# A fused attention and token-MLP kernel on one core: GpSimd library switches moved, head outputs of later query blocks in freed weight space, task order by deadlines

## The chip, the core and the metric

The kernel runs on one core of a Trainium2 chip. The metric is the device time of one execution in microseconds (us). Most executions of one kernel agree within 0.3%; a difference under 2% is called "same".

Engines: TensorE (PE; its weight loads are PEld), VectorE (DVE), ScalarE (ACT), GpSimd (POOL), SyncE (SP, which issues nearly all DMAs). The granted clock is the share of full speed at which TensorE was allowed to run; "half clock" means 0.5.

## The reference

```python
x = A_x                                   # 1 x 2048 x 512, bf16
xn = layernorm(x)                         # over the last axis, no scale
A: qkv = xn @ wqkv; 32 heads of 16; softmax(q k^T / 4) v; then @ wo
B: h = layernorm(xn); u = gelu(h^T @ w1 + b1)   # mixes tokens: 2048 -> 1376
   y = u @ w2 + b2                              # 1376 -> 2048
return x + A + B^T
```

## The kernel before

The kernel is written as a small scheduler. It holds a modelled time for each engine, and picks the next score, exponential, value product or MLP piece by estimate; what it emits is a fixed order of instructions on each engine. So one changed cost or due date moves work everywhere.

The attention has 1024 exponentials of 128x1024. ScalarE does some directly (720 before). VectorE does the others as an integer trick: one pass from PSUM, then three shifted copies, made by VectorE or by GpSimd (`int64_add`). Such an exponential needs four value products on TensorE in place of one.

`affine_select` at the start and `int64_add` in the main loop live in different GpSimd libraries; a switch is put ahead of an instruction whose library may not be resident.

```python
# head: GpSimd
ident.memset(0); affine_select(ident, ...)      # standard library
mhalf.memset(-0.5) ...                          # needed by every rstd (pow)

def late_consts():                              # ahead of the main loop
    pool: memset(wo_t)
    # ... 12 DMAs of wo; those of wo_t wait for the memset
    pool: b1col <- b1c_bf

oT = sb("oT", [128, 2, 4, 512], BF16)           # head outputs, query block % 2

def task_epilogue(b):                           # after the value products of a block
    # ... copy out of PSUM, denominators through DRAM and back to denb
    yield "gate", lambda: qb < 2 or all(("f", 4 * (qb - 2) + i) in have for i in range(4))
    # oT[:, qb % 2, T] = oC32 * denb            # VectorE

# tasks that fill TensorE between scores: Q, K, V projections, MLP in (ut), MLP out (fin)
KV_DUE = {1: BN + 8, 2: 170, 3: 236}            # due = number of the score
for T in range(1, 4):
    for c in range(4):
        ext_tasks.append((KV_DUE[T] - 8, KV_DUE[T] + KV_STEP * c, "kt", ...))
        # ... vt
for i in range(NFT):                            # UT_DUE, UT_STEP = 100, 38
    ext_tasks.append((due - UT_LEAD, due, "ut", ...))
for st in range(NT):                            # FIN_DUE = (500, 650, 800, 920)
    ext_tasks.append((due - 16, due, "fin", ...))
# cuts marked by "..."
```

A Q task ends with eight small DMAs that copy rows of `Qall` into `QT`, and the scores of the next blocks wait for these rows. All these tasks share one PSUM bank.

The softmax here doesn't subtract the row's maximum and nothing guards it: scores larger than these inputs give would overflow.

## Time and profile before

716.44 us (median of 3; 715.01 to 716.99). The profiled execution spans 715.6 us; its device time was 717.96 us, above these three.

| stretch (trace) | us |
|---|---|
| start to the first exponential on ScalarE | 19.86 |
| first to last exponential's start (the loop) | 684.29 |
| last exponential's start to the end (tail) | 11.49 |

Two engines are nearly always busy. These are the first lines of the profile's page (busy us and share of the span, number of instructions), and the chain of waits that ended last, by engine.

```profile
span 715.6 us, 29348 instructions
PE 688.3 (96%) x12863; PEld 315.3 (44%) x12867; DVE 622.7 (87%) x916; ACT 677.8 (95%) x739; POOL 382.6 (53%) x649
PE 67%; ACT 19%; DVE 7%; issue 2%; SPq 2%; POOL 1%; DMA 1%; DVEq 0%; POOLq 0%
```

Busy shares do not say what can be won, so I count starts: back to back, ScalarE starts an exponential every 0.904 us. 719 intervals of that length are 650.0 us, the gelu in the middle of the loop adds 8.1, and 26.2 of the 684.3 us are left. By this count that is what a better order could win at most without moving exponentials.

The head: GpSimd's timeline (start, duration, engine, line, operation, and in brackets the idle time before it with what ended it), then the records of line 396.

```profile
0.72 0.21 POOL L395 MEMSET ident<- 128x128 bf16 x1 [0.30 <-POOLq L1474]
8.72 0.28 POOL L396 TENSOR_SCALAR_AFFINE_SELECT ident<-ident 128x128 bf16<-128x128 bf16 x1 [7.79 <-issue]
8.97 0.09 POOL L399 MEMSET mhalf<- 128x1 f32 x1
```

```profile
L396 POOLq MODIFY_POOL_CONFIG  x2: 11/11/11, 1.1 to 1.2; - x2
```

The library switch itself takes 11 ns at 1.2 us, and then nothing runs on GpSimd for 7.5 us. "Issue" means that the profile shows nothing that was waited for. `mhalf` and all normalization stand behind it.

In the loop, the longest wait of ScalarE for a score (its timeline), and a second place where VectorE's queue stood still for the denominators of an earlier block (VectorE's timeline):

```profile
239.87 2.96 ACT L718 ACTIVATE pT<-ps 128x1024 bf16<-128x1024 f32 x3
247.42 2.13 ACT L718 ACTIVATE pT<-ps 128x1024 bf16<-128x1024 f32 x2 [4.58 <-PE ps L694]
```

```profile
316.15 0.89 DVE L988 TENSOR_TENSOR oT<-oC,denb 128x256 bf16<-128x256 f32 x2 [1.83 <-DMA denb<-rden_scratch]
```

Busy time by stretch around the second (stretch, length, busy us and count of PE, PEld, DVE, ACT, POOL, then granted TensorE clock, DMA share, GB/s):

```profile
315.00:320.00 5.00, 3.37 (x48) 0.88 (x40) 3.78 (x6) 3.19 (x4) 2.47 (x5) 0.90 0.08 20
320.00:325.00 5.00, 5.00 (x88) 2.35 (x88) 3.35 (x6) 3.39 (x4) 1.84 (x3) 0.76 0.05 8
```

TensorE ran dry behind VectorE, its granted clock then fell to half for 3.4 us, and ScalarE lost over 3 us in ten.

### The profile page before, as it was taken

The page shows a single profiled execution, that of the slowest core. Times are in us where ns is not written, and L with a number is a line of the kernel's source. Part 1 is how long each engine was busy: PE and PEld are TensorE (multiplying, and loading weights), DVE is VectorE, ACT ScalarE, POOL GpSimd, SP SyncE. Part 2 cuts the span into 40 slices and gives each one's busy share as a digit, 9 for nine tenths or more (in the row PEclk, how much of TensorE's full clock was granted, in tenths as well). Part 3 has the DMA queues.
Part 4 walks back from the last instruction along what each step waited for, and adds up shares of the span by engine and source line. Part 5 has one row for each costly group of instructions (what it writes and reads, how often), then busy time and mean ns, then how long its engine had stood idle before and what let it go on. Part 6 is the DMA issues. An engine that isn't in the chain of part 4 may idle for free.

```text
span 715.6 us, 29348 instructions
## 1 busy us (share of the span) xinstructions
PE 688.3 (96%) x12863; PEld 315.3 (44%) x12867; DVE 622.7 (87%) x916; ACT 677.8 (95%) x739; POOL 382.6 (53%) x649
## 2 busy tenths in 40 slices
PE   4999999999999999999999999999999999999998
PEld 2544444445444534434444444444444444444444
DVE  3889988998888789888989999997899889898897
ACT  2899999999999799989999999999999999999994
POOL 4454545554544255555656566664656556565662
PEclk7999999999999999999999999999999999999999
DMA  7103020220022121122103211212221222212111
GB/s 208 29 19 66 21 47 19 52 47 17 21 45 43 26 47 39 24 50 40 38 20 74 52 43 40 53 46 51 45 56 35 49 60 51 47 23 56 36 27 44
DMA packets 85728, 32.32 MB, mean 45 GB/s; under 512 B 67424, under 2 KB 85600, under 8 KB 85600
## 3 DMA queue, kind: packets, MB, share of 16 engines
q1 hardware_dynamic: 85168, 30.05, 18.4%
q8 instruction: 101, 1.65, 1.1%
q10 hardware_dynamic: 432, 0.39, 0.2%
q14 instruction: 27, 0.22, 0.1%
HBM read 21.76 MB, written 2.35 MB: 34 GB/s over the span
## 4 chain that ended last, share of the span: by engine, by line
PE 67%; ACT 19%; DVE 7%; issue 2%; SPq 2%; POOL 1%; DMA 1%; DVEq 0%; POOLq 0%
PE ps L761 26%; PE ps L694 24%; PE ps L791 14%; ACT pT L718 13%; ACT x_sb L718 5%; SPq L391 2%; DVE pT L729 2%; PE ps L840 1%; DMA denb<-rden_scratch 1%; DVE x_sb L729 1%; DVE hx L519 1%; ACT gT_sb L895 1%; DVE OT L951 1%; DVE pT L738 0%; DVE oT L988 0%
## 5 line engine op out<-in xcount | busy, mean ns | idle before, releaser
L718 ACT ACTIVATE pT<-ps 128x1024 bf16<-128x1024 f32 x522 | 509.2, 1118 | 9.6 <-PE ps L694 8.5
L694 PE MATMUL ps<-QT,KT 32*128 32x512 bf16 x2048 | 287.5, 385 | 6.5 <-ACT pT L718 2.8
L729 DVE TENSOR_SCALAR pT<-ps 128x1024 int16<-128x1024 f32 x216 | 263.8, 1222 | 28.1 <-PE ps L694 20.6
L735 POOL INT64_ADD pT<-pT x311 | 188.7, 615 | 158.6 <-DVE pT L738 90.8
L761 PE MATMUL ps<-pT,V 128*32 128x256 bf16 x4696 | 251.3, 275 | 2.5 <-DVE OT L951 1.2
L718 ACT ACTIVATE x_sb<-ps 128x1024 bf16<-128x1024 f32 x198 | 210.8, 1122 | 4.2 <-PE ps L694 3.7
L694 PEld LDWEIGHTS ps<-QT,KT 32*128 32x128 bf16 x2048 | 80.8, 91 | 182.5 <-ACT pT L718 69.8
L761 PEld LDWEIGHTS ps<-pT,V 128*32 128x32 bf16 x4696 | 114.5, 96 | 72.4 <-issue 50.9
L761 PE MATMUL ps<-x_sb,V 128*32 128x256 bf16 x1832 | 120.1, 276 | 1.8 <-DVE OT L951 0.8
L729 DVE TENSOR_SCALAR x_sb<-ps 128x1024 int16<-128x1024 f32 x88 | 107.5, 1222 | 9.8 <-PE ps L694 6.7
L735 POOL INT64_ADD pT<-x_sb x117 | 71.3, 617 | 55.4 <-DVE pT L738 40.0
L735 POOL INT64_ADD x_sb<-pT x113 | 69.2, 615 | 57.5 <-DVE pT L738 34.2
L738 DVE TENSOR_SCALAR pT<-pT 128x1024 int16<-128x1024 int16 x154 | 65.6, 428 | 4.6
L761 PEld LDWEIGHTS ps<-x_sb,V 128*32 128x32 bf16 x1832 | 47.4, 96 | 34.0 <-issue 22.9
L761 PE MATMUL ps<-pT,VM 128*32 128x256 bf16 x864 | 61.6, 275 | 0.6 <-DVE pT L738 0.6
L791 PE MATMUL ps<-gT_sb,wblk 128*32 128x512 bf16 (+1 forms) x704 | 60.0, 384 | 0.8 <-DMA wblk<-in_B_w_dram 0.7
L791 PE MATMUL ps<-hx,wblk 128*32 128x512 bf16 x688 | 59.8, 389 | 0.0
L735 POOL INT64_ADD x_sb<-x_sb x49 | 30.1, 618 | 26.8 <-DVE pT L738 15.2
L738 DVE TENSOR_SCALAR x_sb<-pT 128x1024 int16<-128x1024 int16 x70 | 29.7, 427 | 1.9
L738 DVE TENSOR_SCALAR pT<-x_sb 128x1024 int16<-128x1024 int16 x70 | 29.5, 425 | 1.8 <-PE ps L761 0.2
L761 PEld LDWEIGHTS ps<-pT,VM 128*32 128x32 bf16 x864 | 23.3, 96 | 12.4 <-issue 9.5
L761 PE MATMUL ps<-x_sb,VM 128*32 128x256 bf16 x352 | 25.3, 276 | 0.0
(103 smaller groups left out, 385.1 us busy)
## 6 DMA issues: line engine op xcount, KB each, us to landing
wblk<-in_B_w_dram SPq DMA_DIRECT2D x10, 512.0 KB, 4.5
wblk<-in_B_w_dram SPq DMA_DIRECT2D x16, 320.0 KB, 3.7
oC<-OT SPq DMA_DIRECT2D x248, 16.0 KB, 1.8
denb<-rden_scratch SPq DMA_DIRECT2D x124, 32.0 KB, 2.1
xr<-in_A_x_dram SPq DMA_DIRECT2D x16, 128.0 KB, 2.5
dcomp<-OT SPq DMA_DIRECT2D x124, 2.0 KB, 1.8
QT<-Qall SPq DMA_DIRECT2D x120, 16.0 KB, 1.9
out_dram<-osb SPq DMA_DIRECT2D x14, 128.0 KB, 1.8
```

Of the source, the lines that this page charges most:

```text
L391: return eng.dma_start(dst, src)
L519: return [dict(eng="dve", fn=lambda e: e.tensor_scalar(xn_sb[:, t, :], xn_sb[:, t, :], mv[:, t, 3:4], None, ALU.mult), reads=[("xn", t), ( ...
L694: specs.append(dict(eng="pe", fn=lambda e, r=r, bk=bk: e.matmul(bank(bk), lhsT=KT[32 * r:32 * r + 32, T, 128 * kt:128 * (kt + 1)], rhs=QT[ ...
L718: return [dict(eng="act", fn=lambda e: e.activation(buf(pbuf[n]), ps[:, s_ * 1024:(s_ + 1) * 1024], ACTF.Exp, scale=LN2_128), reads=[("ban ...
L729: return dict(eng="dve", fn=lambda e: e.tensor_scalar(buf_i(w), ps[:, s_ * 1024:(s_ + 1) * 1024], IBIAS, 0.0, ALU.add, ALU.max), reads=[(" ...
L735: return dict(eng=eng, fn=lambda e: e.int64_add(buf_i(o).bitcast(I64), buf_i(w).bitcast(I64), SHIFTS[k] * 0x0001000100010001), reads=[("pT ...
L738: return dict(eng=eng, fn=lambda e: e.tensor_scalar(buf_i(o), buf_i(w), float(SHIFTS[k]), 1.0, ALU.add, ALU.mult), reads=[("pT", w)], writ ...
L761: specs.append(dict(eng="pe", fn=lambda e, c=c, h=h, i=i, off=off: e.matmul(bank(PV_BANK)[32 * c:32 * c + 32, 256 * par:256 * par + 256], ...
L791: specs.append(dict(eng="pe", fn=lambda e, c=c, w=w: e.matmul(bank(EX_BANK)[32 * c:32 * c + w, :], lhsT=lhs_of(32 * c, 32 * c + w), rhs=rh ...
L840: specs.append(dict(eng="pe", fn=lambda e, ct=ct, c=c, i=i, t=t: e.matmul(bank(EX_BANK)[32 * c:32 * c + 32, 128 * i:128 * (i + 1)], lhsT=x ...
L895: yield "act", [dict(eng="act", fn=lambda e, ap=ap: e.activation(ap, ap, ACTF.Gelu_apprx_tanh), reads=[("gT", f) for f in fts], writes=[(" ...
L951: yield "pvev", [dict(eng="dve", fn=lambda e: e.tensor_copy(OT32[:, eb, :], bank(PV_BANK)), reads=[("bank", PV_BANK)], writes=[("OT32", eb)])]
```

## The change

The intent: leave the GpSimd with the library that the next execution needs first; do the other switch early; give head outputs of query blocks 2 and 3 their own place (the K and V weights, dead by then), so that they need not wait for the MLP output tasks; and choose the order of tasks from deadlines instead of fixed dates.

```diff
+    def load_lib(lib):
+        sc.add("pool", lambda e: e.load_library(lib), cost=(LIB_I, LIB_I), name="lib", port=False)   # LIB_I = 7.2
     def late_consts():
+        load_lib(INT64_LIB)
         sc.add("pool", lambda e: e.memset(wo_t[:], 0.0), ...)
 ...
-    oT = sb("oT", [128, 2, 4, 512], BF16)
+    oT_a = sb("oT", [128, 2, 4, 512], BF16)
+    oT_b = wkv_raw[:, :].rearrange("p (q t x) -> p q t x", q=2, t=4)
+    def oT(qb): return oT_a[:, qb] if qb < 2 else oT_b[:, qb - 2]
 ...
-    yield "gate", lambda: qb < 2 or all(("f", 4 * (qb - 2) + i) in have for i in range(4))
 ...
+    hard.append((2 * BN * p - Q_LEAD, 0.86, "qt", ...))            # and kt, vt: due = first use - lead
+    soft = [(3.42, "ut", ...)]; fins = [(3.2, "fin", ...)]         # put where the hard ones leave slack
 ...
-D_STEAL = 0.8
-D_LATE = 0.6
+D_STEAL = 0.3
+D_LATE = 1.0
-t_c = max(sc.free["pe"], min(sc.pe_tiles.values()) ...)
+t_c = max(sc.free["pe"], max(sc.pe_tiles.values()) ...)
-late = next_n - cur_ext["due"]                # priority 1 if late > -6 else 3
+late = next_n - min([cur_ext["due"]] + [z[1] - HARD_HOLD for z in ext_tasks if z[2] in ("qt", "kt", "vt")])
+                                               # priority 1 if late > -LATE_BY else 3
 ...
     assert sorted(resid_done) == [0, 1, 2, 3]
+    load_lib(library_config.standard)
     tail()
```

More of the change, by code (lines that the diff above doesn't have):

```diff
@@ L5 @@
 import concourse.bass as bass
+import concourse.bass_isa as bass_isa
+import concourse.library_config as library_config
 from concourse import mybir
@@ L72 @@
 TABLE = 1.3
-KV_STEP = 14
-Q_LEAD = 54
-UT_DUE, UT_STEP = 100, 38
-UT_LEAD = 16
-FIN_DUE = (500, 650, 800, 920)
-FIN_STEP = (32, 32, 28, 24)
+LIB_I = 7.2
+Q_LEAD = 52
+KV_LEAD = 16
+HARD_HOLD = 10
+LATE_BY = 0
+EX_FROM = 34
+EX_RATE = 0.15
+EX_EARLY = 10
+GELU_GAP = 16
 ACT_WIN = 3.42
@@ L354, in bass_parallel_sum__softmax_full_mha__mixer_token_mlp__prompt_kernel, with oT, oT_keys @@
         rcomp = sb("rcomp", [128, 2, 16], F32)
-        oT = sb("oT", [128, 2, 4, 512], BF16)
+        oT_a = sb("oT", [128, 2, 4, 512], BF16)
+        oT_b = wkv_raw[:, :].rearrange("p (q t x) -> p q t x", q=2, t=4)
+        WKV_KEYS = [("wkv", j, T) for j in range(2) for T in range(4)]
+        def oT(qb):
+            return oT_a[:, qb] if qb < 2 else oT_b[:, qb - 2]
+        def oT_keys(qb, T):
+            return [("oTc", qb, T)] + (WKV_KEYS if qb >= 2 else [])
         wblk = sb("wblk", [128, NW, NT, 128], BF16)
@@ L469, in late_consts @@
             sc.add("dve", lambda e: e.memset(gT_sb[FLAST:FLAST + 1, NFT - 1, :], 1.0), writes=[("gTone",)])
+        INT64_LIB = next(z for z in library_config.all_libraries if bass_isa.InstInt64Add in z.tracked_instructions)
+        def load_lib(lib):
+            sc.add("pool", lambda e: e.load_library(lib), cost=(LIB_I, LIB_I), name="lib", port=False)
         def ln_stats(t):
@@ L918, in task_fin @@
                 yield "gate", lambda T=T: (qb, T) in oT_done
-                yield "pe", ext_mm(128, lambda a, z, T=T: oT[:, qb % 2, T, 128 * sti + a:128 * sti + z], wo_c[:, T, :],
-                                   [("oTc", qb % 2, T)] + [("wo_c", e_, r) for e_ in range(2) for r in range(4)],
+                yield "pe", ext_mm(128, lambda a, z, T=T: oT(qb)[:, T, 128 * sti + a:128 * sti + z], wo_c[:, T, :],
+                                   [("oTc", qb, T)] + [("wo_c", e_, r) for e_ in range(2) for r in range(4)],
                                    False, T == ng - 1 and not keep, "op")
@@ L983, in task_epilogue @@
             if half:
-                yield "call", lambda: sc.add("dve", lambda e: e.memset(oT[64:128, qb % 2, T, :], 0.0),
-                                             writes=[("oTc", qb % 2, T)], cost=(0.2, 0.26))
+                yield "call", lambda: sc.add("dve", lambda e: e.memset(oT(qb)[64:128, T, :], 0.0),
+                                             writes=oT_keys(qb, T), cost=(0.2, 0.26))
             for h in range(2):
@@ L988, in task_epilogue @@
                 yield "dve", [dict(eng="dve", fn=lambda e, cs=cs: e.tensor_tensor(
-                    oT[0:m, qb % 2, T, cs], oC32[0:m, tb_, cs], denb[0:m, tb_, cs], ALU.mult),
+                    oT(qb)[0:m, T, cs], oC32[0:m, tb_, cs], denb[0:m, tb_, cs], ALU.mult),
                     reads=[("oC32", tb_, x, c, a) for x in es_ for c in range(4) for a in range(2)] +
                           [("denb", tb_, x, r) for x in es_ for r in range(4)],
-                    writes=[("oTc", qb % 2, T), ("oTh", h)], port=True, cost=(0.33, 0.41))]
+                    writes=oT_keys(qb, T) + [("oTh", h)], port=True, cost=(0.33, 0.41))]
             yield "call", lambda: oT_done.add((qb, T))
@@ L1007, in v @@
                 return ap.rearrange("p (a x) -> p a x", a=2)[:, :, 128 * half:128 * half + 128]
-            t_bf = oT[:, (qb + 1) % 2, :, :].rearrange("p t x -> p (t x)")
+            t_bf = oT(0).rearrange("p t x -> p (t x)")
             oL = t_bf[:, 0:512]
@@ L1025, in tail @@
                 sc.add("dve", lambda e, half=half: e.tensor_tensor(v(oL, half), v(bank(PV_BANK), half), v(oC32[:, tb_, :], half), ALU.mult),
-                       reads=[("bank", PV_BANK), ("rl", half)], writes=[("oTl", half)] + [("oTc", (qb + 1) % 2, z) for z in range(4)] if half == 0 else [("oTl", half)],
+                       reads=[("bank", PV_BANK), ("rl", half)], writes=[("oTl", half)] + [("oTc", 0, z) for z in range(4)] if half == 0 else [("oTl", half)],
                        cost=(0.35, 0.4))
@@ L1030, in heads_of @@
                 sc.add("pe", lambda e: e.matmul(
-                    bank(tbk[sti]), lhsT=oT[:, qb % 2, Tm, 128 * sti:128 * (sti + 1)], rhs=wo_c[:, Tm, :],
+                    bank(tbk[sti]), lhsT=oT(qb)[:, Tm, 128 * sti:128 * (sti + 1)], rhs=wo_c[:, Tm, :],
                     start=Tm == 2 and sti < 3, stop=Tm == 3),
-                    reads=[("oTc", qb % 2, 2) if Tm == 2 else ("oTh", sti // 2)] + wk, writes=[("bank", tbk[sti])])
+                    reads=[("oTc", qb, 2) if Tm == 2 else ("oTh", sti // 2)] + wk, writes=[("bank", tbk[sti])])
             for sti in range(4):
@@ L1093, in bass_parallel_sum__softmax_full_mha__mixer_token_mlp__prompt_kernel @@
         free_p.extend(range(NPB, NPB + NXB))
-        ext_tasks = []
+        hard = []
         for p in range(1, NBLK // 2):
             qb, T = PAIRS[p]
-            b = 2 * p
-            ext_tasks.append((BN * (b - 2) + 2 if b > 2 else 0, BN * b - Q_LEAD, "qt", task_qt(qb, T), None))
-        KV_DUE = {1: BN + 8, 2: 170, 3: 236}
+            hard.append((2 * BN * p - Q_LEAD, 0.86, "qt", task_qt(qb, T), None, 2 * BN * (p - 1) + 2 if p > 1 else 0))
         for T in range(1, 4):
+            n0 = 2 * BN * POS[0, T]
             for c in range(4):
-                ext_tasks.append((KV_DUE[T] - 8, KV_DUE[T] + KV_STEP * c, "kt", task_kt(T, c), None))
-                ext_tasks.append((KV_DUE[T] - 8, KV_DUE[T] + KV_STEP * c + 4, "vt", task_vt(T, c), None))
-        for i in range(NFT):
-            due = UT_DUE + UT_STEP * i
-            ext_tasks.append((due - UT_LEAD, due, "ut", task_ut(i), ("ut", i)))
-        for st in range(NT):
-            due = FIN_DUE[st // 4] + FIN_STEP[st // 4] * (st % 4)
-            ext_tasks.append((due - 16, due, "fin", task_fin(st), ("fin", st)))
+                hard.append((n0 + 8 * c - KV_LEAD, 0.86, "kt", task_kt(T, c), None, 0))
+                hard.append((n0 + 8 * c + 2 - KV_LEAD, 0.96, "vt", task_vt(T, c), None, 0))
+        hard.sort(key=lambda z: z[0])
+        soft = [(3.42, "ut", task_ut(i), ("ut", i)) for i in range(NFT)]
+        fins = [(3.2, "fin", task_fin(st), ("fin", st)) for st in range(NT)]
+        ext_tasks = []
+        cur, k = EX_FROM, 0
+        while hard or soft or fins:
+            tail_ = 0.0
+            slack_ = 1e9
+            for due, cost, *_r in hard:
+                tail_ += cost
+                slack_ = min(slack_, due - cur - tail_ / EX_RATE)
+            nxt = soft[0] if soft else (fins[0] if fins else None)
+            if nxt is not None and (not hard or slack_ > nxt[0] / EX_RATE):
+                cost, nm, gen, need = (soft or fins).pop(0)
+                rel = 0
+            else:
+                due, cost, nm, gen, need, rel = hard.pop(0)
+            cur = max(cur, rel) + cost / EX_RATE
+            ext_tasks.append((max(rel, cur - cost / EX_RATE - EX_EARLY), cur, nm, gen, need))
+            if nm == "ut" and not soft:
+                cur += GELU_GAP
         ext_tasks.sort(key=lambda z: z[1])
@@ L1275, in bass_parallel_sum__softmax_full_mha__mixer_token_mlp__prompt_kernel @@
             t_pe = max(sc.free["pe"], sc.pe_end)
-            t_c = max(sc.free["pe"], min(sc.pe_tiles.values()) if sc.pe_tiles else 0.0) if sc.pe_mode == "C" else t_pe + PE_SWITCH
+            t_c = max(sc.free["pe"], max(sc.pe_tiles.values()) if sc.pe_tiles else 0.0) if sc.pe_mode == "C" else t_pe + PE_SWITCH
             if next_n < NN and pv_block >= next_n // BN - 1 and free_slots and score_has(next_n):
@@ L1290, in bass_parallel_sum__softmax_full_mha__mixer_token_mlp__prompt_kernel @@
             if cur_ext and cur_ext["cur"] and cur_ext["cur"][0] == "pe":
-                late = next_n - cur_ext["due"]
-                jobs.append((max(t_c, est(cur_ext["cur"][1])), 1 if late > -6 else 3, "ext", cur_ext, 0.214))
+                late = next_n - min([cur_ext["due"]] + [z[1] - HARD_HOLD for z in ext_tasks if z[2] in ("qt", "kt", "vt")])
+                jobs.append((max(t_c, est(cur_ext["cur"][1])), 1 if late > -LATE_BY else 3, "ext", cur_ext, 0.214))
             pick = None
```

## The prediction

> **What bounds it now.** 716.4 us: a head of 19.9 us up to the first exponential (timeline of ScalarE), a main loop to about 705, a tail of 10. In the loop (busy time in that stretch) TensorE and ScalarE are 98% busy, VectorE 89%, GpSimd 55%. In the chain of waits TensorE has 67%, ScalarE 19%. ScalarE starts 720 of 1024 exponentials, most of them 0.904 us apart: with about 8 us of gelu its floor for the loop is 659 us, against 685 spent. Of the 26 us above it about 10 are waits for scores (list of waits), one of 4.6 at 247 us, others near 142, 268 and 316-324; the rest is small delays.
>
> **What changes.**
> 1. Library. In the head GpSimd issues its library switch at 1.2 us and its affine select starts at 8.72: 7.8 us idle "issue". The half constant and rstd, and behind them every other engine, stand behind it; the first x tiles had landed by 3.3 us and their statistics were ready by 5. The Trainium skill (GPSIMD Engine Reference, Instruction dispatch) says that the first call to a freshly loaded kernel pays about 6 us without a visible instruction; this trace shows 7.5 between switch and first use. If the previous execution leaves the standard library resident and a switch to a resident library is nearly free, the first exponential comes at about 12 us: 8 us saved, all critical. No trace here shows that such a switch is free: my chance for it is 0.78. The new switch at the end has about 10 us between the last shift and the end and should hide.
> 2. The earlier switch before the loop was hidden already: the first integer add at 57.18 waited for a VectorE shift ending at 57.07. Worth 0. It delays the wo_t loads, and what queues behind them, by up to 7 us: a cost of 0 to 1.
> 3. Order. By static order, the longest stretches of matmuls between two scores were 4.6 us (at score 320; this is the 4.6 us wait), 3.3 and 2.3 (at the gelu, free). After it: 3.0, 2.3, 1.5, all at the gelu; but stretches over 1 us grow from 31 to 44. The separate space for later head outputs removes a gate that I see on no critical wait.
> 4. Balance. ScalarE takes 725 exponentials (+5 x 0.904 = +4.5 us of floor); VectorE 299 (-5 x 1.22) and 32 fewer shifts (-32 x 0.43 = -14), of which GpSimd takes 17; TensorE 15 fewer value products (-1.6) and 8 fewer mode switches (-1).
>
> **Sum.** Head -8; loop +4.5 (floor) -4.6 (the stall) -4 (less VectorE pressure, fewer waits in its queue) +1, about -3 to -5; tail 0. If the library trick fails, about 711.
>
> Predicted 704.5 us, 80% range 698 to 712. Faster by over 2% 0.32, within 2% 0.66, slower 0.02.
>
> **What would show it.** Affine select at about 1.5 us and first exponential at 11-13 us show step 1; an unchanged gap refutes it. Loop of 681-683 us; the 4.6 us wait gone; exponentials still mostly 0.904 apart. Last GpSimd work about 10 us before the end.
>
> **What would make it wrong.** The switch costs the same whatever is resident; the final load holds up the end; a weight or x tile lands later than the earlier head needs it; VectorE stuck behind a late denominator broadcast (1.8 us at 316, TensorE at half clock after it) in new places; or small delays shrink by more than I give the new order, which would carry it over 2%.

## The result, and the profile after

705.38 us (4 runs, 705.33 to 706.08), before 716.31 us over its 4 runs. Ratios here and below are from the fast runs of both kernels in the same rounds, so not quite the ratio of these medians: 0.9852, 95% interval 0.9835 to 0.9869. By the 2% rule this is "same"; it is a clear gain of 1.5%.

| trace | before | after | difference |
|---|---|---|---|
| start to first exponential | 19.86 | 12.95 | -6.9 |
| loop | 684.29 | 677.66 | -6.6 |
| tail | 11.49 | 13.68 | +2.2 |
| exponentials on ScalarE | 720 | 725 | +5 |
| loop: intervals x 0.904 | 650.0 | 654.5 | +4.5 |
| loop: gelu | 8.1 | 8.3 | +0.2 |
| loop: the rest | 26.2 | 14.9 | -11.3 |

The page's first lines and the chain, as before:

```profile
span 704.3 us, 29187 instructions
PE 688.5 (98%) x12808; PEld 325.6 (46%) x12808; DVE 607.0 (86%) x879; ACT 680.4 (97%) x744; POOL 391.3 (56%) x666
PE 73%; ACT 19%; DVE 3%; issue 2%; SPq 2%; POOL 1%; DVEq 0%; DMA 0%; POOLq 0%
```

TensorE's busy time is what it was in a span 11 us shorter: the gain came out of idle time. The chain runs through VectorE and DMA less (3% and 0% in place of 7% and 1%).

The head, GpSimd's timeline and the records of the switch:

```profile
0.72 0.20 POOL L408 MEMSET ident<- 128x128 bf16 x1 [0.29 <-POOLq L1507]
1.42 0.29 POOL L409 TENSOR_SCALAR_AFFINE_SELECT ident<-ident 128x128 bf16<-128x128 bf16 x1 [0.49 <-POOL ident L408]
1.67 0.10 POOL L412 MEMSET mhalf<- 128x1 f32 x1
```

```profile
L409 POOLq MODIFY_POOL_CONFIG  x2: 11/11/11, 1.3 to 1.4; - x2
```

The same two instructions stand there, and the affine select follows in less than 0.1 us. The waits of ScalarE in the loop that its timeline shows (those over 0.15 us) sum to 3.4 us (before: 11.7); the longest are these:

```profile
67.71 12.02 ACT L737 ACTIVATE pT<-ps 128x1024 bf16<-128x1024 f32 x13 [0.82 <-PE ps L713]
94.16 1.02 ACT L737 ACTIVATE x_sb<-ps 128x1024 bf16<-128x1024 f32 x1 [0.68 <-PE ps L713]
677.00 1.94 ACT L737 ACTIVATE pT<-ps 128x1024 bf16<-128x1024 f32 x2 [0.73 <-PE ps L713]
```

The tail is longer because a whole output task now runs behind the last exponential (TensorE's timeline; the last exponential starts at 690.60):

```profile
693.12 2.55 PE L810 MATMUL ps<-gT_sb,wblk 128*32 128x512 bf16 x44
```

And the early switch, on GpSimd's timeline. The memset of wo_t is the first instruction behind it:

```profile
40.19 0.65 POOL L591 TENSOR_SCALAR VM<-V 128x544 bf16<-128x544 bf16 x1 [0.73 <-DVE V L546]
46.41 1.79 POOL L472 MEMSET wo_t<- 128x2048 bf16 x1 [5.58 <-issue]
```

### The profile page after: what moved, and what is told of

It is laid out like the page before. It is cut to its first block, busy times and chain, and to the rows that moved or that the text cites. A ratio compares the mean times of both kernels' runs of the same rounds, so it can differ in the third digit from the quotient of the medians.

```text
span 704.3 us, 29187 instructions
## 1 busy us (share of the span) xinstructions
PE 688.5 (98%) x12808; PEld 325.6 (46%) x12808; DVE 607.0 (86%) x879; ACT 680.4 (97%) x744; POOL 391.3 (56%) x666
## 4 chain that ended last, share of the span: by engine, by line
PE 73%; ACT 19%; DVE 3%; issue 2%; SPq 2%; POOL 1%; DVEq 0%; DMA 0%; POOLq 0%
PE ps L780 27%; PE ps L713 27%; PE ps L810 15%; ACT pT L737 13%; ACT x_sb L737 4%; SPq L404 2%; PE ps L859 1%; DVE pT L748 1%; ACT gT_sb L914 1%; PE ps L619 0%; DVE oT L1006 0%; PE ps L563 0%; PE ps L550 0%; DVE x_sb L748 0%; POOL V L626 0%
## 5 line engine op out<-in xcount | busy, mean ns | idle before, releaser
L737 ACT ACTIVATE pT<-ps 128x1024 bf16<-128x1024 f32 x522 | 515.4, 1151 | 3.8 <-PE ps L713 3.2
L748 DVE TENSOR_SCALAR pT<-ps 128x1024 int16<-128x1024 f32 x207 | 252.9, 1222 | 32.7 <-PE ps L713 23.6
L780 PE MATMUL ps<-pT,V 128*32 128x256 bf16 x4632 | 237.9, 275 | 0.9 <-ACT pT L737 0.6
L737 ACT ACTIVATE x_sb<-ps 128x1024 bf16<-128x1024 f32 x203 | 221.8, 1159 | 1.1 <-PE ps L713 0.9
L713 PEld LDWEIGHTS ps<-QT,KT 32*128 32x128 bf16 x2048 | 86.5, 91 | 179.2 <-ACT pT L737 80.6
L780 PE MATMUL ps<-x_sb,V 128*32 128x256 bf16 x1856 | 115.1, 275 | 0.3 <-ACT x_sb L737 0.3
L754 POOL INT64_ADD pT<-x_sb x128 | 77.4, 613 | 56.8 <-DVE pT L757 32.6
L754 POOL INT64_ADD x_sb<-x_sb x58 | 35.3, 613 | 28.4 <-DVE pT L757 8.1
L810 PEld LDWEIGHTS ps<-hx,wblk 128*32 128x32 bf16 x688 | 16.2, 94 | 24.1 <-issue 21.1
L810 PEld LDWEIGHTS ps<-gT_sb,wblk 128*32 128x32 bf16 (+1 forms) x704 | 16.3, 95 | 20.8 <-issue 16.1
```

The lines of the kernel that those rows point to most:

```text
L713: specs.append(dict(eng="pe", fn=lambda e, r=r, bk=bk: e.matmul(bank(bk), lhsT=KT[32 * r:32 * r + 32, T, 128 * kt:128 * (kt + 1)], rhs=QT[ ...
L737: return [dict(eng="act", fn=lambda e: e.activation(buf(pbuf[n]), ps[:, s_ * 1024:(s_ + 1) * 1024], ACTF.Exp, scale=LN2_128), reads=[("ban ...
L748: return dict(eng="dve", fn=lambda e: e.tensor_scalar(buf_i(w), ps[:, s_ * 1024:(s_ + 1) * 1024], IBIAS, 0.0, ALU.add, ALU.max), reads=[(" ...
L754: return dict(eng=eng, fn=lambda e: e.int64_add(buf_i(o).bitcast(I64), buf_i(w).bitcast(I64), SHIFTS[k] * 0x0001000100010001), reads=[("pT ...
L780: specs.append(dict(eng="pe", fn=lambda e, c=c, h=h, i=i, off=off: e.matmul(bank(PV_BANK)[32 * c:32 * c + 32, 256 * par:256 * par + 256], ...
L810: specs.append(dict(eng="pe", fn=lambda e, c=c, w=w: e.matmul(bank(EX_BANK)[32 * c:32 * c + w, :], lhsT=lhs_of(32 * c, 32 * c + w), rhs=rh ...
```

## The experiments

Twelve runs were made (one of them the kernel after once more), in three calls, each call on one chip. Before in the same rounds was 716.08, 716.64 and 716.32 us.

| run | us (median) | ratio to before | 95% interval | first exp. | loop | tail |
|---|---|---|---|---|---|---|
| restore_only | 708.02 | 0.9884 | 0.9870 to 0.9899 | 12.74 | 682.1 | 11.5 |
| no_restore | 715.08 | 0.9981 | 0.9966 to 0.9997 | 21.80 | 677.8 | 13.7 |
| no_early | 704.56 | 0.9841 | 0.9824 to 0.9858 | 12.66 | 676.3 | 13.7 |
| no_space | 708.38 | 0.9888 | 0.9873 to 0.9903 | 12.39 | 674.5 | 18.6 |
| no_order | 727.47 | 1.0135 | 1.0092 to 1.0178 | 12.82 | 696.9 | 14.6 |
| no_tune | 712.80 | 0.9915 | 0.9857 to 0.9973 | 13.04 | 683.2 | 15.2 |
| warm17 | 704.27 | 0.9810 | 0.9768 to 0.9852 | 11.61 | 677.1 | 13.7 |
| best | 705.38 | 0.9827 | 0.9784 to 0.9870 | 11.61 | 677.6 | 13.7 |
| old_order_tune | 715.67 | 0.9988 | 0.9968 to 1.0008 | 12.45 | 688.3 | 12.7 |
| space_alone | 708.52 | 0.9885 | 0.9863 to 0.9907 | 13.50 | 682.3 | 11.5 |
| after_again | 705.36 | 0.9844 | 0.9825 to 0.9863 | 11.74 | 677.2 | 13.7 |
| cand_tc | 716.16 | 1.0000 | 0.9975 to 1.0025 | 11.61 | 686.2 | 15.4 |

All gave correct results. The three last columns are of one profiled execution each.

### 1. Is the head's gap the library? restore_only and no_restore

```diff
# restore_only: the kernel before
     assert sorted(resid_done) == [0, 1, 2, 3]
+    sc.add("pool", lambda e: e.load_library(library_config.standard), ...)
     tail()
# no_restore: the kernel after
-    load_lib(library_config.standard)
```

> The kernel before, with only the switch back to the standard library added behind the last integer add. Theory (the head's gap is the load of a library that the previous execution had left swapped out): affine select at about 1.4 us instead of 8.7, first exponential 6.9 us earlier (about 13.0), the rest of the trace as before, time 709.3 (708.5 to 710.5), ratio to before 0.990. Rival (the gap went with the new schedule or the second early switch, and the switch back costs its 5 to 7 us at the end): affine select still at 8.7, or a tail longer by 5 us; time 716 or more.

Measured: 708.02 us, affine select at 1.43 us, first exponential 7.1 us earlier, tail 11.49 as before, so the last switch hides. The loop was 2.2 us shorter than in the profile of before although the order is the same: here the half clock at 319 us did not occur.

> The kernel after without the switch back at the end; every other instruction the same. Theory: the 7.3 us gap before the affine select returns, first exponential at about 19.9, time 712.3 (711.5 to 713.5). Rival: no gap, time 705.4, because the last load was not what removed it. Tail from the last exponential's start stays at 13.7 us in theory; if it shortens, the final load had held up the end.

Measured: 715.08 us, 9.7 more than after, where I expected 6.9. The loop and tail are as in after (677.8 and 13.7): the profiled executions differ by 9.0 us, and 8.9 of these are in the head. The time from the switch to the first use was longer than in before:

```profile
L409 POOLq MODIFY_POOL_CONFIG  x2: 11/11/11, 1.2 to 1.2; - x2
L409 POOL TENSOR_SCALAR_AFFINE_SELECT ident<-ident x1: 283/283/283, 10.5 to 10.5; 128x128 bf16<-128x128 bf16 x1
```

That is 9.3 us, against 7.5 in before and 5.5 for the early switch in after. The DMA engines were busy to 0.93, 0.84 and 0.00 of those three stretches. That the switch loads something, and that this competes with the weight loads, fits these three numbers; but no run varied the DMA load alone, and in the 5.5 us of the early switch the traced queues moved one packet of 0.01 MB, so the load itself is not seen among them. It is argued, not shown.

Both runs say the same from two sides: the state of the library outlives the execution, and putting it back takes 8 to 10 us off the time. The rival is out. No run put another kernel in between: the gain is shown only for executions as they were timed here.

### 2. The early switch: no_early

```diff
     def late_consts():
-        load_lib(INT64_LIB)
```

> The kernel after without the explicit switch ahead of the main loop; the switch then stands just before the first integer add, as in the kernel before, and the scheduler does not count it (723 exponentials on ScalarE, 301 on VectorE, all else nearly the same order). Theory: worth nothing, 705.4 give or take 1.5. Rival: the switch in front of the first shift costs: the first integer add and what waits for it come 2 to 5 us late, time 707 to 710.

Measured: 704.56 us, and 2 fewer exponentials on ScalarE (723). The interval overlaps that of after; the theory (worth nothing) holds in this order, and the rival is out. Below, the pair warm17 and best repeats it on one chip with the sign reversed: 704.27 with the early switch, 705.38 without. One thing differs in the traces: both profiled executions without it (no_early and best) have 3.4 us of half clock from about 49 us on, behind short waits of TensorE, and those of after, after_again and warm17 have none there.

### 3. The separate space: no_space and space_alone

```diff
# no_space: the kernel after
-    def oT(qb): return oT_a[:, qb] if qb < 2 else oT_b[:, qb - 2]
+    def oT(qb): return oT_a[:, qb % 2]
+    yield "gate", lambda: qb < 2 or all(("f", 4 * (qb - 2) + i) in have for i in range(4))
# space_alone: the kernel before with restore_only's line and the new space, no gate
```

> The kernel after with two slots of head outputs and their gate again, order and tuning as in after. By static order the matmuls behind the last score are 10.6 us in place of 5.6 (kernel before: 3.6). Theory: without the space the last output tasks are pushed behind the last score, so the tail from the last exponential grows by 4 to 5 us and the time is 709 to 710.5. Rival (as I predicted: the gate was on no critical wait): 705.4 give or take 1.

Measured: 708.38 us, +3.0 (the ratios 0.9888 and 0.9844 to 0.9852 do not overlap in their intervals). The tail grew by 4.9 us as the theory said, and its loop is 3.1 us shorter, which fits work that only moved behind it. Behind its last exponential (686.92 us) TensorE's timeline shows more than two whole output tasks where after has one:

```profile
687.74 1.47 PE L808 MATMUL ps<-gT_sb,wblk 128*32 128x512 bf16 x24
690.45 2.55 PE L808 MATMUL ps<-gT_sb,wblk 128*32 128x512 bf16 x44
694.36 2.55 PE L808 MATMUL ps<-gT_sb,wblk 128*32 128x512 bf16 x44
```

> The kernel before plus the switch back at the end and the separate space, order and tuning as before. By static order TensorE's work is placed as in the switch-back-alone run, and 3.6 us lie behind the last score in both. Theory (the space is worth something only where the order leaves output tasks for the end): 708.0 give or take 1. Rival (the space is worth its 3 us by itself): 705.

Measured: 708.52 us, against 708.02 of restore_only; the theory holds. The space is worth 3 us in the new order and nothing in the former one.

### 4. The order and the tuning: no_order, no_tune, old_order_tune

```diff
# no_order: the former ext_tasks with KV_DUE, UT_DUE, FIN_DUE, and "late > -6"
# no_tune: D_STEAL 0.8, D_LATE 0.6, t_c with min(...)
# old_order_tune: both
```

> The kernel after with the former fixed due dates and lateness rule of the MLP, Q, K and V tasks; library, space, tuning constants as in after. By static order there are then 11.6 us of matmuls between two scores at score 320 (plus 2.7 behind them) and 6.4 behind the last score; in after the long ones lie at the gelu. Theory (the new order's worth is that ScalarE does not run dry): one ScalarE wait of 8 to 11 us near 235 us, time 711 to 715. Rival (TensorE is the limit, so the order within it costs nothing): ScalarE's wait is made up at the end, time within 2 us of 705.4.

Measured: 727.47 us, 22 more than after and worse than I expected. The wait is there, but it is 17.2 us long, not 8 to 11, with another of 4.1 behind it:

```profile
252.59 1.02 ACT L737 ACTIVATE x_sb<-ps 128x1024 bf16<-128x1024 f32 x1 [17.21 <-PE ps L713]
257.74 1.02 ACT L737 ACTIVATE x_sb<-ps 128x1024 bf16<-128x1024 f32 x1 [4.13 <-PE ps L713]
```

My 11.6 us counted matmuls only. In these 17 us TensorE ran two K tasks, a Q task, two V tasks and a whole MLP task one after the other, and between them waited for VectorE to empty their one PSUM bank; one such piece of its timeline (the first two of the rows that this score needs had landed by 243.6 us, so here the work in front held it):

```profile
243.17 1.05 PE L810 MATMUL ps<-xnT,wkv_raw 128*32 128x512 bf16 x16 [0.80 <-DVE V L868]
245.02 1.08 PE L859 MATMUL ps<-wkv_raw,xnT 128*32 128x128 bf16 x64 [0.80 <-DVE KT L849]
246.90 3.64 PE L810 MATMUL ps<-hx,wblk 128*32 128x512 bf16 x64 [0.80 <-DVE V L868]
```

The rival (made up at the end) is out.

> The kernel after with the former constants for handing exponentials to VectorE and the former estimate of when TensorE is free; order, space, library as in after. 721 exponentials on ScalarE, 1933 value products (+12, about +1.3 us of TensorE) and 8.3 us of matmuls behind the last score in place of 5.6. Theory: the tuning moves exponentials but the time little: 706 to 707.5, tail 2 to 3 us longer, loop 1 to 2 shorter. Rival (less VectorE pressure was worth the 4 us that I predicted): 709 or more, with many small waits for VectorE.

Measured: 712.80 us with a wide spread, 709.8 to 714.7. The time fits the rival's number more than mine, but not by many small waits. In the profiled execution, the slowest of the four, the tail grew by 1.5 us and the loop, which I expected to shrink, by 5.5. One event stands out, ten us in which ScalarE was idle for 3.25: VectorE waited 1.8 us for late denominators, TensorE ran dry, and then ran at half clock for 6.8 us:

```profile
135.00:140.00 5.00, 3.29 (x54) 1.39 (x54) 3.16 (x6) 3.00 (x4) 1.69 (x3) 0.90 0.18 31
140.00:145.00 5.00, 5.00 (x60) 1.46 (x52) 2.66 (x5) 3.75 (x4) 2.87 (x6) 0.50 0.11 23
```

It is the same kind of event as at 316 us in before. Neither theory named it, so this run does not decide between them.

> The kernel after with both the former task dates and the former tuning: the kernel before plus the library's two switches and the separate space. Theory (order and tuning only work as a pair, tuned together; the former pair had its own 4.6 us wait): 708 to 712, that is the switch-back-alone run (708.0) with one ScalarE wait of 5 to 8 us, now at score 384, waiting for the copied Q rows. Rival (the new order is worth the 22 us of the run with the former dates alone): 720 or more.

Measured: 715.67 us, over the range of my theory and under the rival's. The expected wait is there, 6.65 us long. These are the MLP task in front of the score, the weight loads of this score (284.41) and of the next one (284.66), and ScalarE:

```profile
280.74 3.63 PE L810 MATMUL ps<-hx,wblk 128*32 128x512 bf16 x64
284.41 0.10 PEld L713 LDWEIGHTS ps<-QT,KT 32*128 32x128 bf16 x2 [0.32 <-issue]
284.66 0.09 PEld L713 LDWEIGHTS ps<-QT,KT 32*128 32x128 bf16 x1 [0.16 <-DMA QT<-Qall]
284.84 1.94 ACT L737 ACTIVATE pT<-ps 128x1024 bf16<-128x1024 f32 x2 [6.65 <-PE ps L713]
```

The profile names the Q rows for the next score only. For this one the two rows that it needs were issued at 280.71 and 281.26 us and landed 2.9 and 2.7 us later, by 284.0; it ran 0.4 us after that. So with this Q task the wait could have been at most 0.4 us shorter. The MLP task in front ends at 284.4 as well; the trace does not say which of the two alone would have held the score less.

A half clock of 6.8 us from 291 us follows. Against space_alone (708.5) it differs only in the early switch and its modelled 7.2 us, and is 7 us slower. The early switch was worth nothing in section 2; here it shifted the scheduler's choices (723 exponentials on ScalarE in place of 720), and the wait for the Q rows and the half clock behind it are longer. That these two are the whole of the 7 us is not shown. Such a number belongs to the order that came out, not to the ingredient.

### 5. The head's last microsecond: warm17, best, after_again

```diff
# warm17: the kernel after;  best: the same without the early switch
-N_WARM = 11
+N_WARM = 17
```

> The kernel after with 17 warm-up matmuls in place of 11, so that TensorE is busy from 1.2 us to about 7, when the transposes come. Theory (the head gave 6.9 us instead of 8 because TensorE, idle from 5.7 to 7.0 us, ran at half clock from 8.7 to 12): clock 1.0 from 8 to 12 us, first exponential 0.7 to 1.5 us earlier (11.5 to 12.2), time 704.0 to 704.7. Rival (the head waits for x tiles, statistics and evictions, not for TensorE): first exponential at 12.9, time 705.4.

Measured: first exponential at 11.61 us, clock 1.0 throughout, 704.27 us. Busy time by stretch in after and in warm17 (clock is the third number from the end):

```profile
8.00:10.00 2.00, 1.38 (x15) 1.21 (x14) 1.94 (x4) 1.05 (x3) 0.87 (x4) 0.67 1.01 340
10.00:12.00 2.00, 2.00 (x22) 2.00 (x20) 0.77 (x2) 0.46 (x2) 0.81 (x2) 0.50 1.05 342
```

```profile
8.00:10.00 2.00, 1.38 (x24) 1.21 (x23) 1.97 (x5) 1.40 (x3) 0.89 (x4) 1.00 1.08 366
10.00:12.00 2.00, 1.90 (x33) 1.50 (x31) 1.43 (x4) 0.86 (x2) 0.81 (x2) 1.00 1.07 344
```

> Candidate: the kernel after without the early switch and with 17 warm-up matmuls. If the 0.8 us of the run without the early switch and the 1 us of the longer warm-up are both real and add up: 703.2 to 704.2, faster than both kernels. If the warm-up does nothing: 704.6.

Measured: 705.38 us. Its head is the same 11.61; its loop is no shorter. The two parts did not add up: the 0.8 us of no_early did not repeat. Its trace has two half-clock stretches of 3.4 us in the loop (from 48.5 and 174.8 us), that of warm17 none; what they cost was not measured.

> The kernel after once more, as the control for this chip: 705.4 give or take 0.8, first exponential at 12.7 to 13.0.

Measured: 705.36 us, but its profiled execution had no half clock in the head and its first exponential at 11.74, outside what I expected. So with 11 warm-up matmuls the head's clock differs from one execution to the next. Of the nine profiled heads with 11 warm-ups and the library in place eight ran partly at half clock, and the first exponential came at 11.74 to 13.50 us; with 17 none of three did, and it came at 11.61 in each.

warm17 beats the kernel before clearly (0.981; by the 2% rule "unclear", since the interval includes 0.98). Against after its 1.1 us is about what the heads differ by, but the intervals overlap and the chips differ, so as a gain in time it is not shown.

### 6. A candidate that failed: cand_tc

```diff
# warm17, with the former estimate
-t_c = max(sc.free["pe"], max(sc.pe_tiles.values()) ...)
+t_c = max(sc.free["pe"], min(sc.pe_tiles.values()) ...)
```

> Candidate: after with 17 warm-up matmuls and with the former estimate of when TensorE is free (earliest instead of latest tile), which in this order leaves no stretch over 1.4 us between two scores but 6.6 us behind the last (after: 5.6). If the head's 1.3 us holds and fewer long stretches help: 702.5 to 704. If only the head counts: 704 to 704.5, tail 1 us longer, loop as long as in after.

Measured: 716.16 us, 12 more than warm17, though its static order looked better. VectorE's waits (engine, line, tile, what was waited for: us in total, times, longest):

```profile
DVE wkv_raw L1006 <- DMA denb<-rden_scratch: 6.4, 3, 3.7
DVE oT L1006 <- DMA denb<-rden_scratch: 5.5, 5, 2.6
```

In after the same two sum to 3.2 us with 1.2 the longest. TensorE was at half clock from 402.0 to 408.8 us. How the 9 us of longer loop divide between these waits, the clock and the rest I have not measured. Lengths of matmul stretches, which had looked better here, do not show a queue standing behind a DMA.

## Why the prediction was right

The time (705.4 against 704.5) and the class came out, and so did the sum's main term. That the total fits to 0.9 us is in part luck, since errors cancelled: in the profiles the head gave 1.1 us less than predicted, the tail cost 2.2 us that the sum did not have, and the loop gave 1.6 to 3.6 us more, of which 2.2 are a half clock that only the profile of before had. Point by point:

1. **Library, -8.** Right in mechanism, shown by restore_only and no_restore; the free switch to a resident library was the open chance, and it is free (under 0.1 us). In size the profile of after gave 6.9 and not 8: TensorE fell to half clock in the head and the first exponential came at 12.95, not about 12; after_again, without the half clock, gave 8.1. My fallback "about 711" was too low: no_restore measured 715.1. Of the 4.1 us that are missing, the longer gap (9.3 in place of 7.5 us) gives 1.8, and 1.5 are my own inconsistency: 704.5 plus the 8 us of the head is 712.5.
2. **Early switch, 0 with a cost of 0 to 1.** Right in the new order: 704.6 without it, and the other sign in the second pair. In the former order the run with it was 7 us slower (old_order_tune against space_alone), which I had not foreseen.
3. **Order.** Right that the 4.6 us wait goes. Wrong, by the trace, in taking it for a stretch of matmuls: the score ran behind two Q rows. In before, `Qall` was written at 242.18 us; the first two row copies, which are those that this score reads, were issued from 242.90 on and landed about 3 us later, by 246.3, and the score ran at 246.99. These are the two copies (issue, then landing), and the last work in front of the score:

```profile
L391 SPq DMA_DIRECT2D QT<-Qall x2: 512/552/591, 242.9 to 243.4; - x2
DMA to landing us min/median/max: 2.9/3.0/3.2
```

```profile
246.65 0.41 PE L840 MATMUL ps<-wkv_raw,xnT 128*32 128x128 bf16 x16 [0.58 <-DVE KT L830]
246.99 0.39 PE L694 MATMUL ps<-QT,KT 32*128 32x512 bf16 x2
```

   So matmuls placed elsewhere could have won at most 0.7 us of the 4.6: the rows were not there before. In after, where Q, K and V tasks have deadlines, no wait is over 0.82 us. No run moved this Q task alone, so this is read from traces.
4. **"A gate that I see on no critical wait."** This step failed. The gate was harmless in the former order (space_alone), but in the new order it pushes output tasks behind the last score: 3.0 us and 4.9 us of tail (no_space). I judged it by the trace of before instead of by the order of after.
5. **Loop -3 to -5, tail 0.** Measured -6.6 and +2.2. The +4.5 us of floor for five more exponentials came out. The rest fell by 11.3 us where I had 4.6 + 4 - 1. Of these 11.3 us, 8.3 are ScalarE's waits for scores (11.7 before, 3.4 after): 4.6 is the stall that I had counted by itself, and 3.4 are the three waits from 318 to 324 us, behind the late denominators and the half clock. The other 3.0 are smaller delays. So about half of the 6.7 us beyond the stall came from one named event; how much general VectorE pressure adds was not separated. And about 2 of the 6.6 us vary from one execution to the next: restore_only and space_alone, in the order of before, had loops of 682.1 and 682.3 us without that half clock. Against these the new loop is 4.4 to 4.6 us shorter, which is inside my -3 to -5. The tail grew by a task that no longer fitted into the loop.

So of the 10.9 us, the switch back at the end gives 8.1 by itself (restore_only against before in the same rounds), and order, tuning, space and early switch together the remaining 2 to 3. Taking single ones of them out of after changes the time by -0.8 us (no_early) to +22 us (no_order). These numbers do not add up; the pieces were tuned together.

## What to carry to other kernels

State that an engine keeps across executions is part of the kernel: an unexplained idle time right behind a switch at the start can be the price of how the last execution ended, and it may be paid where the engine is idle anyway. Where a scheduler decides the order, test each part with the others in place and also without them, and judge a gate by the order that will come out. When a short wait costs more than its length, look at the granted clock in the microseconds after it.

## What the Trainium skill lacked or had wrong

- GPSIMD Engine Reference, Instruction dispatch, gives approximately 6 us (5.95) for the first call to a freshly loaded kernel. The traces agree with the DMA engines idle (5.4 to 5.7 us from switch to memset in the nine traces with the early switch, at DMA shares of at most 0.01) and show more with them busy: 7.5 and 9.3 us at DMA shares of 0.84 and 0.93. It does not say that the loaded library stays for the next execution, nor that a switch to the resident one costs nothing: under 0.1 us in after. It speaks of the first call of the loaded kernel; here a plain memset behind the switch waited as well (5.5 us in after).
- TensorE: Matmul & The Clock Gate, What's actually happening, has a free-running window of 3413 ns; the traces agree (half-clock stretches of 3.4, 6.8 and 10.2 us, and the same head with and without one). It says that the half clock comes after at least one idle window of about 3.4 us; a later section of the page (A second HAM failure mode) tells of short idle times bringing it on in another kernel. Here seven half-clock stretches inside the loops began without an idle window: TensorE had been busy for 1.7 to 2.4 of the 3.41 us before each. In before it was busy for 1.78 us, with one idle time of 1.63 us from 316.6 us on, and half clock came at 319.0 us. Busy time alone does not decide it: in no_order 1.65 busy us of 3.41, from 254.2 us on, were followed by full clock.
